# The first feed-forward product by Strassen's algorithm: seven block products per pair of channel tiles and batch in place of eight

## The chip, the cores and the metric

The kernel runs on one core of a Trainium2 chip. The metric is device time in microseconds (us) of one execution; a lower time is better. The engines are named PE (TensorE; PEld is its weight load), DVE (VectorE), ACT (ScalarE), POOL (GpSimd) and SP (SyncE, which issues the DMAs).

## What is computed

Three blocks follow each other: a clustered attention, a first mixing block and a second one, which is where the change lies. With `x` of 2 batches x 768 positions x 512 channels, the second block is

```python
h = xt @ U @ V                      # xt = x transposed, rank 32
u = x + h.transpose(0, 2, 1)
ch = np.maximum(u @ w_ch1, 0.0) @ w_ch2     # 512 -> 2048 -> 512
return u + ch
```

## The kernel before

Everything is kept transposed: channels lie on the 128 partitions, positions along the free axis. `xT[b * 4 + t]` is channel tile t (128 of the 512 channels) of batch b, 768 columns of fp32. Products are made in three passes: each operand is split into a high part `hi` (rounded to fp32r by ACT) and a remainder `lo` (by DVE or POOL), and `PASSES` multiplies hi by hi, hi by lo and lo by hi into the same PSUM bank. Weights come as 64-bit floats. A `Convert` loads 768 columns (SP), makes the fp32 value from the two words (one ACT and three DVE operations: `magnitude`, `bits`, `top`, `low`), and `keep_split` splits it (`wh` on ACT, `wl` on POOL). `conv_step()` emits one DVE operation of the current conversion and one pending function of a finished one; `conv_until` goes on until a given tile is there.

No scheduler reorders the work: each engine takes its instructions in the order of the program text, and waits in that order. PSUM has 8 banks, handed out in turn by `bank()`; a bank is written again only when the reader of its last content is done. SBUF tiles of 128x768 fp32 come from a pool of `SLOTS`.

The stage around the change is the end of `mixer()`. After `chmix(1, e)` and `turn(1, e)` (the last product of the first mixing block and a transposition on DVE), `low1(b)` makes `xt @ U` (24 matmuls, then four ACT copies, a DVE cast and subtraction, which give `h1s`), `low2(b, t)` adds `h` to `xT` (8 matmuls and 8 DVE adds per batch), and `split_u` splits u for the feed-forward products. The loop over `fs` then runs 4 groups of 4 channel tiles f of the 2048, 3 chunks of 512 of the 1536 columns, and 4 tiles f inside. `ff1(c, f)` makes one tile of `u @ w_ch1` (12 matmuls of 512 columns, or 24 of 256 in the chunk that spans both batches), ReLU and the split into `gh` (ACT) and `gl` (DVE). `ff2(c, f)`, two steps later, multiplies it by `w_ch2` into four kept banks, and every fourth f `ff_sum` adds these to `xT`; the last sums go to the output.

Of the kernel before, what the change touches and what calls it, by code (L numbers as in the profile page):

```python
# [10 lines left out]
F32 = mybir.dt.float32  # L11
# [11 lines left out]
P = 128  # L23
NP = 4
# [5 lines left out]
INV_2PI = 1.0 / TWO_PI  # L30
SIN_SCALE = float(np.nextafter(np.float32(TWO_PI), np.float32(0)))
MAGIC = 1.5 * 2.0 ** 23
SLOTS = 62
SETS = 3
STAGED = 3

# [5 lines left out]
def tile_cluster_block(ctx: ExitStack, tc: tile.TileContext, qk, v, cent, wth, wr, wi, wch,  # L42
# [321 lines left out]
    class Convert:  # L364


        def __init__(self, src, n, i, done, rows=P, copies=1):
            self.src, self.i, self.rows, self.copies = src, i, rows, copies
            self.done, self.t = done, None
            self.c0, self.w = i * S, min(S, n - i * S)  # L370

        def load(self):
            self.st = stg.tile([P, S, 2], I32, tag="st", name="st")
# [73 lines left out]
    def weigh_in(src, n, dst):  # L447
        return [Convert(src, n, i, keep_split(dst)) for i in range((n + S - 1) // S)]

    wth_t, wch_t, wr_t, wi_t, w1_t, w2_t = {}, {}, {}, {}, {}, {}  # L450

    def wcol(tiles, c, n):
        i, o = divmod(c, S)
# [156 lines left out]
                             start=True, stop=True)  # L610
            nc.vector.tensor_tensor(x[:, cols(hf)], ps[:, :HALF], x[:, cols(hf)], op=ALU.add)

    def split_u(b, t):
        x = xT[b * NP + t]
        hi, lo = slot(f"uh{b}{t}", F32R), slot(f"ul{b}{t}", F32R)
        nc.scalar.activation(out=hi, in_=x, func=AF.Copy)
        (nc.gpsimd if t % 2 else nc.vector).tensor_tensor(lo, x, f32(hi), op=ALU.subtract)
        us[b, t] = (hi, lo)


    CHUNKS = [[(0, 0, 512)], [(0, 512, 256), (1, 0, 256)], [(1, 256, 512)]]
    NF = DFF // P
    GF = 4
    gt, aps = {}, {}

    def ff1(c, f):
        ps = bank("g")
        o = 0
        for b, s0, w in CHUNKS[c]:
            n = 0  # L630
            for t in range(NP):
                wv = wcol(w1_t, (f * NP + t) * P, P)
                for a, e in PASSES:
                    nc.tensor.matmul(out=ps[:, o:o + w], lhsT=wv[a], rhs=us[b, t][e][:, s0:s0 + w],  # L634
                                     start=(n == 0), stop=(n == 11))
                    n += 1
            o += w
        gh = tmp.tile([P, 512], F32R, tag="gh", name="gh")
        nc.scalar.activation(out=gh, in_=ps, func=AF.Relu)  # L639
        gl = tmp.tile([P, 512], F32R, tag="gl", name="gl")  # L640
        nc.vector.scalar_tensor_tensor(gl, ps, 0.0, f32(gh), op0=ALU.max, op1=ALU.subtract)  # L641
        gt[c, f] = (gh, gl)

    def ff2(c, f):
        first, last = f % GF == 0, f % GF == GF - 1
        if first:
            for e in range(4):
                aps[c, e] = bank("acc", f"acc{e}")
        g = gt.pop((c, f))
        end = last and f == NF - 1  # L650
        for e in range(4):
            wv = wcol(w2_t, f * DM + e * P, P)
            for i, (a, x) in enumerate(PASSES):
                nc.tensor.matmul(out=aps[c, e], lhsT=wv[a], rhs=g[x],  # L654
                                 start=(first and i == 0), stop=(last and i == 2))
            if last:
                ff_sum(c, e, end)

    def ff_sum(c, e, end):

        p0 = 0
        for b, s0, w in CHUNKS[c]:
            x = xT[b * NP + e][:, s0:s0 + w]
            nc.vector.tensor_tensor(x, aps[c, e][:, p0:p0 + w], x, op=ALU.add)
            if end:
                t0 = b * S + s0
                nc.sync.dma_start(out=out[e * P:(e + 1) * P, t0:t0 + w], in_=x)
            p0 += w
        give(f"acc{e}")
# [204 lines left out]
    def mixer():  # L874

        seq = [(u, st) for u in range(4) for st in range(NT)]
        LEAD = 2
        CONVERT = (*range(3, 16), 20, 21)
        last = NG - 1
        for n in range(len(seq) + LEAD):  # L880
            if n < len(seq):
                theta(*seq[n])
                if 3 <= n < 22:
                    conv_step()
                theta_z(*seq[n])
            if n >= LEAD:
                ymix(*seq[n - LEAD])
            if n == 1:
                row_sums(last)
            if n == 2:  # L890
                spread(last)
                norm_x(last)
            if n in CONVERT:
                conv_step()
            if n < len(seq):
                theta_lo(*seq[n])
            if n in CONVERT:
                conv_step()
            if n in (9, 10):
                for t in range(2):  # L900
                    split_x(1, 2 * (n - 9) + t)
            if n == 11:
                conv_load.extend(weigh_in(wch, NP * DM, wch_t))
                c1, c2 = weigh_in(w1, NF * DM, w1_t), weigh_in(w2, NF * DM, w2_t)
                ff = [c for p in zip(c1, c2) for c in p]
                conv_load.extend(ff[:5])
                conv_load.append(Convert(u_in, S, 0, [lambda c, g=g: keep_u(c, g) for g in range(4)], 32, 4))
                conv_load.append(Convert(v_in, S, 0, [keep_v, keep_vl], 32))
                conv_load.extend(ff[5:])
                conv_start()  # L910
            if 20 <= n <= 23:
                clear_u(n - 20)
                split_x(0, n - 20)
            if n in (24, 25):
                split_x(1, n - 24, nc.gpsimd)

        for e in range(NP):
            chmix(0, e)
            if e in (0, 1):
                split_x(1, 2 + e)  # L920
            turn(0, e)
            conv_step(3 if e < 2 else 2)
        conv_until(uv, "u")
        conv_until(uv, "v")
        chmix(1, 0)
        turn(1, 0)
        low1(0)
        chmix(1, 1)
        for t in range(NP):
            low2(0, t)  # L930
        turn(1, 1)
        for t in range(NP):
            split_u(0, t)
        chmix(1, 2)
        turn(1, 2)
        chmix(1, 3)
        turn(1, 3)
        fs = [(c, f) for k in range(NF // GF) for c in range(3) for f in range(k * GF, k * GF + GF)]
        AHEAD = 2
        for n in range(len(fs) + AHEAD):  # L940
            if n < len(fs):
                ff1(*fs[n])
            if n == 0:
                low1(1)
            if n in (1, 2):
                low2(1, 2 * n - 2)
                low2(1, 2 * n - 1)
            if n in (1, 2):
                for t in range(2):
                    split_u(1, 2 * n - 2 + t)  # L950
            conv_step(1 + n % 2 if n > 2 else 0)
            if n >= AHEAD:
                ff2(*fs[n - AHEAD])

    with tc.manual_schedule():
        prologue()
# [7 lines left out]
def _layout(i):  # L964
# [17 lines left out]
    a["wch"] = rows(i["moe_w_ch"])  # L982
    a["u"] = c(i["moe2_U"].reshape(24, 32, RANK).transpose(1, 0, 2).reshape(32, -1))
    a["v2"] = c(i["moe2_V"])
    a["w1"] = c(i["moe2_w_ch1"].reshape(NP, P, DFF // P, P).transpose(1, 2, 0, 3).reshape(P, -1))
    a["w2"] = rows(i["moe2_w_ch2"])
    for k in _WIDE:
        a[k] = a[k].view(np.int64)
    cst = np.zeros((P, 160), np.float32)
# [21 lines left out]
```

## Time and profile before

| | |
|---|---|
| time, median of 3 runs | 698.63 us (697.76 to 699.19) |
| profiled execution: its own time | 697.8 us |
| profiled execution: span of its instructions | 696.0 us |
| mean granted clock of PE | 0.994 |
| instructions | 11370 |

The span runs from the first to the last instruction; some 1.8 us of the time lie around it. A granted clock of 1.00 is 2.4 GHz, 0.50 is 1.2 GHz. PE's matmuls overlap, so that a group's time is read from the start of its first to the start of the next group, not from the duration of one.

### The profile page before, as it was taken

What the parts mean: (1) busy time and instruction counts of PE and PEld (TensorE: products, weight loads), DVE (VectorE), ACT (ScalarE), POOL (GpSimd) and SP (SyncE); (2) the same over time, 40 slices, a digit from 0 to 9 for tenths busy, and PEclk for the clock granted to TensorE, in tenths of its full rate; (3) what the DMA queues carried; (4) which work ended last, traced back from release to release, by engine and by line L of the source; (5) the groups of instructions that cost most, each with busy time, mean ns of one, the idle gap of its engine ahead of it and who ended that gap; (6) DMA issues with size and microseconds to landing.
All of it is one profiled execution on the core that took longest, in us unless ns stands there. A gap on an engine that the chain in (4) does not pass through costs nothing.

```text
span 696.0 us, 11370 instructions
## 1 busy us (share of the span) xinstructions
PE 681.6 (98%) x4492; PEld 556.6 (80%) x4492; DVE 452.1 (65%) x752; ACT 301.8 (43%) x617; POOL 181.0 (26%) x186
## 2 busy tenths in 40 slices
PE   8899999999998999999999999999999999999997
PEld 3567676656755599999999998888898889888986
DVE  7888889898997465568684985566554656432222
ACT  8648557657659444555455432322222222211110
POOL 9422313313228331123244121212121212100000
PEclk9899999999999999999999999999999999999999
DMA  6769768557324110013220320112222121000111
GB/s 211 192 148 288 211 172 229 170 149 203 124 91 137 46 31 2 1 46 103 80 58 1 96 86 1 47 46 90 59 79 89 48 76 31 1 1 0 61 49 72
DMA packets 21109, 63.11 MB, mean 91 GB/s; under 512 B 4192, under 2 KB 6112, under 8 KB 21056
## 3 DMA queue, kind: packets, MB, share of 16 engines
q1 hardware_dynamic: 21056, 62.39, 31.0%
q8 instruction: 35, 0.57, 0.3%
q14 instruction: 18, 0.15, 0.1%
HBM read 40.94 MB, written 3.15 MB: 63 GB/s over the span
## 4 chain that ended last, share of the span: by engine, by line
PE 87%; ACT 5%; DVE 4%; DMA 2%; SPq 1%; issue 1%; ACTq 0%
PE g L634 19%; PE acc L654 19%; PE y L520 14%; PE pv L316 8%; PE st L303 6%; PE h L538 5%; PE th L478 5%; PE l L335 4%; PE smax L251 3%; ACT p L308 2%; DVE mx L255 2%; PE h L589 2%; DMA raw<-in_qk_dram 1%; PE th L482 1%; ACT hi L188 1%
## 5 line engine op out<-in xcount | busy, mean ns | idle before, releaser
L405 POOL TENSOR_TENSOR wl<-cv,wh 128x768 fp32r<-128x768 f32 (+1 forms) x40 | 79.1, 1978 | 235.7 <-ACT wh L401 206.2
L641 DVE SCALAR_TENSOR_TENSOR gl<-g,gh 128x512 fp32r<-128x512 f32 x48 | 33.1, 689 | 133.1 <-ACT gh L639 133.0
L639 ACT ACTIVATE gh<-g 128x512 fp32r<-128x512 f32 x48 | 28.7, 599 | 206.1 <-PE g L634 206.1
L255 DVE TENSOR_REDUCE mx<-smax 128x1 f32<-128x512 f32 x144 | 89.6, 681 | 16.4 <-PE smax L251 16.4
L308 ACT ACTIVATE p<-st 128x512 f32<-128x512 f32 x192 | 78.9, 514 | 43.3 <-PE st L303 42.0
L520 PE MATMUL y<-wh,z 128*128 128x384 f32 x384 | 87.6, 340 | 0.3 <-ACT z L498 0.3
L634 PE MATMUL g<-uh,wh 128*128 128x512 f32 (+1 forms) x256 | 86.9, 339 | 0.0
L634 PE MATMUL g<-uh,wl 128*128 128x512 f32 (+1 forms) x256 | 86.5, 338 | 0.0
L634 PE MATMUL g<-ul,wh 128*128 128x512 f32 (+1 forms) x256 | 86.0, 336 | 0.0
L303 PE MATMUL st<-qp,kp 128*128 128x256 f32 (+1 forms) x384 | 78.7, 349 | 0.4 <-ACT qp L284 0.2
L654 PE MATMUL acc<-gh,wh 128*128 128x512 f32 x192 | 75.9, 395 | 0.0
L654 PE MATMUL acc<-gh,wl 128*128 128x512 f32 x192 | 75.5, 393 | 0.0
L654 PE MATMUL acc<-gl,wh 128*128 128x512 f32 x192 | 75.3, 392 | 0.0
L303 PEld LDWEIGHTS st<-qp,kp 128*128 128x128 f32 x384 | 58.6, 192 | 17.3 <-issue 4.1
L520 PEld LDWEIGHTS y<-wh,z 128*128 128x128 f32 x384 | 66.9, 188 | 0.5 <-ACT z L498 0.5
L316 PE MATMUL pv<-p,v 128*32 128x384 f32 x768 | 65.5, 486 | 0.0
L392 DVE SCALAR_TENSOR_TENSOR cv<-st,cv 128x768 int32<-128x768 int32 (+2 forms) x42 | 64.5, 1537 | 1.0
L316 PEld LDWEIGHTS pv<-p,v 128*32 128x32 f32 x768 | 31.6, 110 | 30.1 <-issue 21.6
L634 PEld LDWEIGHTS g<-ul,wh 128*128 128x128 f32 x256 | 48.5, 189 | 6.1
L634 PEld LDWEIGHTS g<-uh,wl 128*128 128x128 f32 x256 | 48.4, 189 | 5.8
L634 PEld LDWEIGHTS g<-uh,wh 128*128 128x128 f32 x256 | 48.4, 189 | 5.7
L520 PE MATMUL y<-wl,z 128*128 128x384 f32 x192 | 48.8, 335 | 0.0
(128 smaller groups left out, 1166.4 us busy)
## 6 DMA issues: line engine op xcount, KB each, us to landing
st<-in_w_dram SPq DMA_DIRECT2D x20, 768.0 KB, 4.2
raw<-in_qk_dram SPq DMA_DIRECT2D x16, 384.0 KB, 4.5
qp<-hi SPq DMA_DIRECT2D x26, 192.0 KB, 2.9
st<-in_wr_dram SPq DMA_DIRECT2D x6, 768.0 KB, 4.9
st<-in_wi_dram SPq DMA_DIRECT2D x6, 768.0 KB, 4.4
kp<-hi SPq DMA_DIRECT2D x32, 96.0 KB, 3.1
qp<-lo SPq DMA_DIRECT2D x32, 96.0 KB, 2.9
v<-in_v_dram SPq DMA_DIRECT2D x8, 384.0 KB, 3.5
```

What stands on the lines that cost most here:

```text
L255: nc.vector.tensor_reduce(mx_t[g, h][:, o:o + n], ps.rearrange("p (n w) -> p n w", n=n), axis=AX.X, op=ALU.max)
L303: nc.tensor.matmul(out=ps[:, c:c + n], lhsT=kp[s, h, w][:, (a + j) * P:(a + j + 1) * P], rhs=qp[s, h, w][:, q0:q0 + n], start=(w == 0), st ...
L308: nc.scalar.activation(out=pt[g, h, a + j][:, q0:q0 + n], in_=ps[:, c:c + n], func=AF.Exp, scale=float(D) ** -0.5)
L316: nc.tensor.matmul(out=pvt[g][hf][r:r + 32, :HALF], lhsT=v_t[g][:, kt, r:r + 32], rhs=pt[g, r // 64, kt][:, cols(hf)], start=(kt == 0), st ...
L392: nc.vector.scalar_tensor_tensor(t, self.hw, SIGN, t, op0=ALU.bitwise_and, op1=ALU.bitwise_or)
L405: nc.gpsimd.tensor_tensor(t[:, :c.w], c.t, f32(c.hi[:, :c.w]), op=ALU.subtract)
L478: nc.tensor.matmul(out=ps[:, 1], lhsT=xs[b, t][a][:, st * P:(st + 1) * P], rhs=wv[c], start=(n == 0), stop=(n == 11))
L520: nc.tensor.matmul(out=yps[u, j][hf][:, :HALF], lhsT=lhs, rhs=w[st][e][:, hf * HALF:(hf + 1) * HALF], start=(st == 0 and n == 0), stop=(st ...
L538: nc.tensor.matmul(out=ps[hf][:, :HALF], lhsT=wv[a], rhs=xs[b, t][c][:, hf * HALF:(hf + 1) * HALF], start=(n == 0), stop=(n == 11))
L634: nc.tensor.matmul(out=ps[:, o:o + w], lhsT=wv[a], rhs=us[b, t][e][:, s0:s0 + w], start=(n == 0), stop=(n == 11))
L641: nc.vector.scalar_tensor_tensor(gl, ps, 0.0, f32(gh), op0=ALU.max, op1=ALU.subtract)
L654: nc.tensor.matmul(out=aps[c, e], lhsT=wv[a], rhs=g[x], start=(first and i == 0), stop=(last and i == 2))
```

## The change

The operands of the first feed-forward product are cut in two along each axis: the 512 input channels (tiles 0, 1 and tiles 2, 3), the output channels (a pair of tiles f) and the 768 positions of a batch (two halves of 384). A 2x2 by 2x2 block product takes eight block products; the algorithm (in its form with fifteen additions) takes seven, of sums and differences of blocks.

- Weights: `weigh_pair(k)` loads the two tiles of pair k as two conversions of 512 columns, forms the sums s1 to s4 on POOL, and splits them (`keep_22`, `sums`, `keep_upper`, `keep_lower`).
- Activations: `u_sum(b, i)` forms t1 to t4 on DVE, `split_sum` splits them; `split_left` and `split_down` split the blocks of u that are used as they are. `split_u` goes.
- Products: a `Quartet(k, b)` has seven `step`s, each one block product (6 matmuls of 384 columns into one bank) and the additions on DVE that assemble the four blocks of g; `keep` does ReLU and the high part on ACT and the remainder on POOL. Its eight `unit`s are the second product, 6 matmuls of 384 columns each, added to `xT` by DVE after every unit.
- Order: the steps of one quartet alternate with the units of the one before. The first quartet starts between the `chmix` of batch 1; the splits of batch 1 come after its last step, its units after those.
- `_layout` orders the weights in DRAM to match, and the pool has 63 slots for 62.

The diff, without the blank lines and without the removed functions that are printed above:

```diff
--- before.py
+++ after.py
@@ -30,7 +30,7 @@
 INV_2PI = 1.0 / TWO_PI
 SIN_SCALE = float(np.nextafter(np.float32(TWO_PI), np.float32(0)))
 MAGIC = 1.5 * 2.0 ** 23
-SLOTS = 62
+SLOTS = 63
 SETS = 3
 STAGED = 3
@@ -364,10 +364,10 @@
     class Convert:
-        def __init__(self, src, n, i, done, rows=P, copies=1):
+        def __init__(self, src, n, i, done, rows=P, copies=1, width=S):
             self.src, self.i, self.rows, self.copies = src, i, rows, copies
             self.done, self.t = done, None
-            self.c0, self.w = i * S, min(S, n - i * S)
+            self.c0, self.w = i * width, min(width, n - i * width)
         def load(self):
             self.st = stg.tile([P, S, 2], I32, tag="st", name="st")
@@ -380,7 +380,8 @@
         def magnitude(self):
-            self.t = slot("cv")[self.part, :self.w]
+            self.tile = slot("cv")
+            self.t = self.tile[self.part, :self.w]
             nc.scalar.activation(out=self.t, in_=self.hw.bitcast(F32), func=AF.Abs, scale=REBIAS)
         def bits(self):
@@ -447,7 +448,53 @@
     def weigh_in(src, n, dst):
         return [Convert(src, n, i, keep_split(dst)) for i in range((n + S - 1) // S)]
-    wth_t, wch_t, wr_t, wi_t, w1_t, w2_t = {}, {}, {}, {}, {}, {}
+    wth_t, wch_t, wr_t, wi_t, w2_t = {}, {}, {}, {}, {}
+    w1_t, lower = {}, {}
+    def weigh_pair(k):
+        Q = 2 * P
+        def part(c, i):
+            return c.tile[:, i * Q:(i + 1) * Q]
+        def keep_22(c):
+            lower[k] = c
+            t = slot("w22", F32R)
+            nc.scalar.activation(out=t[:, :Q], in_=part(c, 1), func=AF.Copy)
+            nc.gpsimd.tensor_tensor(t[:, Q:2 * Q], part(c, 1), f32(t[:, :Q]), op=ALU.subtract)
+            nc.gpsimd.tensor_tensor(part(c, 2), part(c, 0), part(c, 1), op=ALU.add)
+            lower[k, 22] = t
+        def sums(u):
+            c = lower[k]
+            nc.gpsimd.tensor_tensor(part(u, 2), part(c, 2), part(u, 0), op=ALU.subtract)
+            nc.gpsimd.tensor_tensor(part(c, 0), part(u, 0), part(c, 0), op=ALU.subtract)
+            nc.gpsimd.tensor_tensor(part(c, 1), part(u, 1), part(u, 2), op=ALU.subtract)
+        def split(t):
+            hi = slot("wh", F32R)
+            nc.scalar.activation(out=hi, in_=t, func=AF.Copy)
+            lo = slot("wl", F32R)
+            nc.gpsimd.tensor_tensor(lo, t, f32(hi), op=ALU.subtract)
+            return hi, lo
+        def keep_upper(u):
+            x = split(u.tile)
+            for i, nm in enumerate(("11", "12", "s2")):
+                lower[k, nm] = [t[:, i * Q:(i + 1) * Q] for t in x]
+        def keep_lower(u):
+            x, t = split(lower[k].tile), lower[k, 22]
+            got = {nm: [t[:, i * Q:(i + 1) * Q] for t in x] for i, nm in enumerate(("s3", "s4", "s1"))}
+            got.update({nm: lower[k, nm] for nm in ("11", "12", "s2")})
+            got["22"] = [t[:, :Q], t[:, Q:2 * Q]]
+            w1_t[k] = got
+        n = NF * DM
+        return [Convert(w1, n, 2 * k, [keep_22], width=DM),
+                Convert(w1, n, 2 * k + 1, [sums, keep_upper, keep_lower], width=DM)]
     def wcol(tiles, c, n):
         i, o = divmod(c, S)
@@ -610,63 +657,121 @@
                              start=True, stop=True)
             nc.vector.tensor_tensor(x[:, cols(hf)], ps[:, :HALF], x[:, cols(hf)], op=ALU.add)
...
+    def split_part(b, t, c, hi, lo, eng):
+        x = xT[b * NP + t][:, c]
         nc.scalar.activation(out=hi, in_=x, func=AF.Copy)
...
+        eng.tensor_tensor(lo, x, f32(hi), op=ALU.subtract)
+    def split_left(b):
+        hi, lo = [slot(f"u{b}11{e}", F32R, [P, 2, HALF]) for e in range(2)]
+        for j in range(2):
+            split_part(b, j, cols(0), hi[:, j], lo[:, j], nc.gpsimd)
+        us[b, "11"] = hi, lo
+    def split_down(b, j):
+        if j == 0:
+            us[b, "21"], us[b, "22"] = ({}, {}), ({}, {})
+        hi, lo = slot(f"uh{b}{j}", F32R), slot(f"ul{b}{j}", F32R)
+        split_part(b, 2 + j, slice(0, S), hi, lo, nc.gpsimd)
+        for hf in range(2):
+            for e, t in enumerate((hi, lo)):
+                us[b, f"2{hf + 1}"][e][j] = t[:, cols(hf)]
+    ut = {}
+    def u_sum(b, i):
+        t = slot(f"t{i}", F32, [P, 2, HALF])
+        for j in range(2):
+            up, down = xT[b * NP + j], xT[b * NP + 2 + j]
+            p, m = {1: lambda: (up[:, cols(1)], up[:, cols(0)]), 2: lambda: (down[:, cols(1)], ut[b, 1][:, j]),
+                    3: lambda: (down[:, cols(1)], up[:, cols(1)]), 4: lambda: (down[:, cols(0)], ut[b, 2][:, j])}[i]()
+            nc.vector.tensor_tensor(t[:, j], p, m, op=ALU.subtract)
+        ut[b, i] = t
+    def split_sum(b, i, eng):
+        hi, lo = [slot(f"u{b}t{i}{e}", F32R, [P, 2, HALF]) for e in range(2)]
+        t = ut[b, i]
+        nc.scalar.activation(out=hi, in_=t, func=AF.Copy)
+        eng.tensor_tensor(lo, t, f32(hi), op=ALU.subtract)
+        us[b, f"t{i}"] = hi, lo
     NF = DFF // P
...
+    NQ = NF // 2
+    class Quartet:
+        def __init__(self, k, b):
+            self.k, self.b, self.g = k, b, {}
+        def products(self, ps, x, y):
+            conv_until(w1_t, self.k)
+            w, u = w1_t[self.k][x], us[self.b, y]
             n = 0
...
+            for j in range(2):
                 for a, e in PASSES:
...
+                    nc.tensor.matmul(out=ps[:, :HALF], lhsT=w[a][:, j * P:(j + 1) * P], rhs=u[e][j] if type(u[e]) is dict else u[e][:, j],
+                                     start=(n == 0), stop=(n == 5))
                     n += 1
...
+        def temp(self, i):
+            return tmp.tile([P, 512], F32R, tag=("gh", "gl")[i], name="sum").bitcast(F32)[:, :HALF]
+        def add(self, out, ps, x):
+            nc.vector.tensor_tensor(out, ps[:, :HALF], x, op=ALU.add)
+        def keep(self, i, hf, r):
+            t = slot("g", F32R, [P, 2, HALF])
+            nc.scalar.activation(out=r, in_=r, func=AF.Relu)
+            nc.scalar.activation(out=t[:, 0], in_=r, func=AF.Copy)
+            nc.gpsimd.tensor_tensor(t[:, 1], r, f32(t[:, 0]), op=ALU.subtract)
+            self.g[i, hf] = t
+        def step(self, n):
+            x, y = (("11", "11"), ("12", "21"), ("s2", "t2"), ("s3", "t3"), ("s1", "t1"), ("22", "t4"), ("s4", "22"))[n]
+            ps = bank("q")
+            self.products(ps, x, y)
+            if n == 0:
+                self.u1 = self.temp(0)
+                nc.scalar.activation(out=self.u1, in_=ps[:, :HALF], func=AF.Copy)
+            elif n == 1:
+                r = self.temp(1)
+                self.add(r, ps, self.u1)
+                self.keep(0, 0, r)
+            elif n == 2:
+                self.add(self.u1, ps, self.u1)
+            elif n == 3:
+                self.u2 = self.temp(0)
+                self.add(self.u2, ps, self.u1)
+            elif n == 4:
+                r = self.temp(1)
+                self.add(r, ps, self.u2)
+                self.add(self.u1, ps, self.u1)
+                self.keep(1, 1, r)
+            elif n == 5:
+                self.add(self.u2, ps, self.u2)
+                self.keep(1, 0, self.u2)
+            else:
+                self.add(self.u1, ps, self.u1)
+                self.keep(0, 1, self.u1)
+        def unit(self, n):
+            hf, e = divmod(n, NP)
+            ps = bank("acc")
+            m = 0
+            for i in range(2):
+                wv = wcol(w2_t, (2 * self.k + i) * DM + e * P, P)
+                for a, x in PASSES:
+                    nc.tensor.matmul(out=ps[:, :HALF], lhsT=wv[a], rhs=self.g[i, hf][:, x],
+                                     start=(m == 0), stop=(m == 5))
+                    m += 1
+            x = xT[self.b * NP + e][:, cols(hf)]
+            self.add(x, ps, x)
+            if self.k == NQ - 1:
+                t0 = self.b * S + hf * HALF
+                nc.sync.dma_start(out=out[e * P:(e + 1) * P, t0:t0 + HALF], in_=x)
     bg = deque()
@@ -901,8 +1006,12 @@
                     split_x(1, 2 * (n - 9) + t)
             if n == 11:
                 conv_load.extend(weigh_in(wch, NP * DM, wch_t))
-                c1, c2 = weigh_in(w1, NF * DM, w1_t), weigh_in(w2, NF * DM, w2_t)
-                ff = [c for p in zip(c1, c2) for c in p]
+                c2 = weigh_in(w2, NF * DM, w2_t)
+                ff = []
+                for k in range(NQ):
+                    ff.extend(weigh_pair(k))
+                    while c2 and c2[0].c0 < (k + 1) * 2 * DM:
+                        ff.append(c2.pop(0))
                 conv_load.extend(ff[:5])
                 conv_load.append(Convert(u_in, S, 0, [lambda c, g=g: keep_u(c, g) for g in range(4)], 32, 4))
                 conv_load.append(Convert(v_in, S, 0, [keep_v, keep_vl], 32))
@@ -929,28 +1038,55 @@
         for t in range(NP):
             low2(0, t)
         turn(1, 1)
-        for t in range(NP):
-            split_u(0, t)
+        split_left(0)
+        for j in range(2):
+            split_down(0, j)
         chmix(1, 2)
         turn(1, 2)
+        q = Quartet(0, 0)
+        q.step(0)
+        for i in (1, 2):
+            u_sum(0, i)
         chmix(1, 3)
         turn(1, 3)
-        fs = [(c, f) for k in range(NF // GF) for c in range(3) for f in range(k * GF, k * GF + GF)]
-        AHEAD = 2
-        for n in range(len(fs) + AHEAD):
-            if n < len(fs):
-                ff1(*fs[n])
-            if n == 0:
-                low1(1)
-            if n in (1, 2):
-                low2(1, 2 * n - 2)
-                low2(1, 2 * n - 1)
-            if n in (1, 2):
-                for t in range(2):
-                    split_u(1, 2 * n - 2 + t)
-            conv_step(1 + n % 2 if n > 2 else 0)
-            if n >= AHEAD:
-                ff2(*fs[n - AHEAD])
+        split_sum(0, 2, nc.vector)
+        for i in (3, 4):
+            u_sum(0, i)
+        for i, eng in ((3, nc.gpsimd), (1, nc.vector), (4, nc.gpsimd)):
+            split_sum(0, i, eng)
+        q.step(1)
+        low1(1)
+        q.step(2)
+        q.step(3)
+        for t in range(NP):
+            low2(1, t)
+        for n in (4, 5, 6):
+            q.step(n)
+        split_left(1)
+        for j in range(2):
+            split_down(1, j)
+        for i in (1, 2, 3, 4):
+            u_sum(1, i)
+            split_sum(1, i, nc.vector if i < 3 else nc.gpsimd)
+        for n in range(8):
+            q.unit(n)
+        was = None
+        for k in range(NQ):
+            for b in range(2):
+                if k == b == 0:
+                    continue
+                q = Quartet(k, b)
+                for n in range(7):
+                    q.step(n)
+                    if was:
+                        was.unit(n)
+                    if 0 < n < (7 if k == 0 else 6):
+                        conv_step()
+                if was:
+                    was.unit(7)
+                was = q
+        for n in range(8):
+            was.unit(n)
     with tc.manual_schedule():
         prologue()
@@ -982,8 +1118,9 @@
     a["wch"] = rows(i["moe_w_ch"])
     a["u"] = c(i["moe2_U"].reshape(24, 32, RANK).transpose(1, 0, 2).reshape(32, -1))
     a["v2"] = c(i["moe2_V"])
-    a["w1"] = c(i["moe2_w_ch1"].reshape(NP, P, DFF // P, P).transpose(1, 2, 0, 3).reshape(P, -1))
-    a["w2"] = rows(i["moe2_w_ch2"])
+    half = DFF // P // 2
+    a["w1"] = c(i["moe2_w_ch1"].reshape(NP, P, 2, half, P)[:, :, ::-1].transpose(1, 3, 2, 0, 4).reshape(P, -1))
+    a["w2"] = c(i["moe2_w_ch2"].reshape(2, half, P, DM).transpose(2, 1, 0, 3).reshape(P, -1))
     for k in _WIDE:
         a[k] = a[k].view(np.int64)
     cst = np.zeros((P, 160), np.float32)
```

## Rows read from the trace of the kernel before

**Rows 1.** The page, part 1: busy us (share of the span), instructions.

```profile
PE 681.6 (98%) x4492; PEld 556.6 (80%) x4492; DVE 452.1 (65%) x752; ACT 301.8 (43%) x617; POOL 181.0 (26%) x186
```

**Rows 2.** The page, part 4: the chain that ended last, by engine.

```profile
PE 87%; ACT 5%; DVE 4%; DMA 2%; SPq 1%; issue 1%; ACTq 0%
```

**Rows 3.** Windows: stretch, us, busy PE, PEld, DVE, ACT, POOL, clock, DMA, GB/s.

```profile
417.50:435.00 17.50, 17.50 (x105) 15.60 (x104) 10.01 (x24) 5.08 (x10) 1.85 (x1) 1.00 0.00 1
...
500.00:525.00 25.00, 25.00 (x145) 21.94 (x144) 15.24 (x18) 6.74 (x10) 4.17 (x2) 1.00 0.20 64
```

**Rows 4.** The chain in order of time: start us, us, what.

```profile
403.37 4.16 PE h L538 x24
407.53 1.45 PE h L609 x8
...
417.88 2.76 PE g L634 x12
420.64 5.36 PE h L589 x48
...
441.17 2.88 PE g L634 x24
...
463.85 2.76 PE g L634 x12
```

**Rows 5.** Timeline of the end: start us, us, engine, line, what.

```profile
691.85 0.40 PE L654 MATMUL acc<-gh,wl 128*128 128x512 f32 x1
```

**Rows 6.** Groups by line, weight loads: shape, count | busy us, mean ns.

```profile
L634 PEld LDWEIGHTS g<-ul,wh 128*128 128x128 f32 x256 | 48.5, 189 | 6.1
```

**Rows 7.** Single lines: duration ns min/median/max, starts, shapes.

```profile
L611 DVE TENSOR_TENSOR xT<-h,xT x16: 544/546/548, 408.4 to 435.4; 128x384 f32<-128x384 f32 x16
L392 DVE SCALAR_TENSOR_TENSOR cv<-st,cv x42: 685/959/2491, 73.5 to 608.9; 128x768 int32<-128x768 int32 x37, 128x512 int32<-128x512 int32 x4, 32x768 int32<-32x768 int32 x1
L465 DVE TENSOR_TENSOR xl<-xT,xh x10: 946/951/958, 288.0 to 387.5; 128x768 fp32r<-128x768 f32 x10
L504 POOL TENSOR_TENSOR z<-tht,z x24: 732/738/1274, 242.8 to 371.8; 128x256 fp32r<-128x256 f32 x24
L193 POOL TENSOR_TENSOR lo<-raw,hi x16: 1812/1834/1970, 6.5 to 163.1; 128x768 fp32r<-128x768 f32 x16
L498 ACT ACTIVATE z<-tht x48: 399/410/421, 242.0 to 371.3; 128x256 fp32r<-128x256 f32 x48
L401 ACT ACTIVATE wh<-cv x40: 616/837/922, 78.4 to 617.6; 128x768 fp32r<-128x768 f32 x36, 128x512 fp32r<-128x512 f32 x4
```

**Rows 8.** Timeline of DVE ahead of the feed-forward stage.

```profile
408.40 3.80 DVE L611 TENSOR_TENSOR xT<-h,xT 128x384 f32<-128x384 f32 x8
...
413.19 3.44 DVE L617 TENSOR_TENSOR ul<-xT,uh 128x768 fp32r<-128x768 f32 x2
...
419.45 1.13 DVE L554 STREAM_TRANSPOSE xt<-xT 128x192 f32<-128x192 f32 x4
...
427.18 0.41 DVE L598 CAST h1s<-h 32x512 fp32r<-32x512 f32 x1 [5.18 <-ACT h L595]
427.63 0.68 DVE L599 TENSOR_TENSOR h1s<-h,h1s 32x512 fp32r<-32x512 f32 x1
```

**Rows 9.** Timeline of ACT, two places.

```profile
371.60 2.30 ACT L463 ACTIVATE xh<-xT 128x768 fp32r<-128x768 f32 x3
...
426.04 1.11 ACT L595 ACTIVATE h<-h 32x128 f32<-32x128 f32 x4 [4.76 <-PE h L589]
```

**Rows 10.** Timeline of POOL beside rows 8.

```profile
411.36 4.44 POOL L617 TENSOR_TENSOR ul<-xT,uh 128x768 fp32r<-128x768 f32 x2 [21.24 <-ACT uh L616]
```

**Rows 11.** Windows near the start, columns as in rows 3.

```profile
15.00:20.00 5.00, 3.74 (x14) 1.69 (x14) 4.69 (x11) 3.37 (x6) 4.94 (x4) 0.90 1.01 319
20.00:25.00 5.00, 4.71 (x18) 3.53 (x19) 3.99 (x7) 2.81 (x6) 4.95 (x8) 0.50 0.96 207
25.00:30.00 5.00, 5.00 (x35) 3.05 (x33) 4.72 (x12) 3.70 (x9) 0.03 (x1) 0.92 0.90 253
```

More of the change, by code (lines that the diff above doesn't have):

```diff
@@ L611, in low2 @@
             nc.vector.tensor_tensor(x[:, cols(hf)], ps[:, :HALF], x[:, cols(hf)], op=ALU.add)
-    def split_u(b, t):
-        x = xT[b * NP + t]
-        hi, lo = slot(f"uh{b}{t}", F32R), slot(f"ul{b}{t}", F32R)
+    def split_part(b, t, c, hi, lo, eng):
+        x = xT[b * NP + t][:, c]
         nc.scalar.activation(out=hi, in_=x, func=AF.Copy)
-        (nc.gpsimd if t % 2 else nc.vector).tensor_tensor(lo, x, f32(hi), op=ALU.subtract)
-        us[b, t] = (hi, lo)
-    CHUNKS = [[(0, 0, 512)], [(0, 512, 256), (1, 0, 256)], [(1, 256, 512)]]
@@ L622, in tile_cluster_block @@
-    NF = DFF // P
[L623 to L629, printed above, removed]
+        eng.tensor_tensor(lo, x, f32(hi), op=ALU.subtract)
[12 more added lines that the diff above has]
+                us[b, f"2{hf + 1}"][e][j] = t[:, cols(hf)]
@@ L630, in ff1 @@
+    NF = DFF // P
+    NQ = NF // 2
[5 more added lines that the diff above has]
+            w, u = w1_t[self.k][x], us[self.b, y]
             n = 0
-            for t in range(NP):
-                wv = wcol(w1_t, (f * NP + t) * P, P)
+            for j in range(2):
                 for a, e in PASSES:
-                    nc.tensor.matmul(out=ps[:, o:o + w], lhsT=wv[a], rhs=us[b, t][e][:, s0:s0 + w],
-                                     start=(n == 0), stop=(n == 11))
+                    nc.tensor.matmul(out=ps[:, :HALF], lhsT=w[a][:, j * P:(j + 1) * P], rhs=u[e][j] if type(u[e]) is dict else u[e][:, j],
+                                     start=(n == 0), stop=(n == 5))
@@ L636, in ff1 @@
                     n += 1
[L637 to L669, printed above, removed]
+        def temp(self, i):
+            return tmp.tile([P, 512], F32R, tag=("gh", "gl")[i], name="sum").bitcast(F32)[:, :HALF]
@@ L931, in mixer @@
         turn(1, 1)
-        for t in range(NP):
-            split_u(0, t)
+        split_left(0)
+        for j in range(2):
+            split_down(0, j)
         chmix(1, 2)
         turn(1, 2)
+        q = Quartet(0, 0)
+        q.step(0)
+        for i in (1, 2):
+            u_sum(0, i)
         chmix(1, 3)
         turn(1, 3)
-        fs = [(c, f) for k in range(NF // GF) for c in range(3) for f in range(k * GF, k * GF + GF)]
-        AHEAD = 2
-        for n in range(len(fs) + AHEAD):
-            if n < len(fs):
-                ff1(*fs[n])
-            if n == 0:
-                low1(1)
-            if n in (1, 2):
-                low2(1, 2 * n - 2)
-                low2(1, 2 * n - 1)
-            if n in (1, 2):
-                for t in range(2):
-                    split_u(1, 2 * n - 2 + t)
-            conv_step(1 + n % 2 if n > 2 else 0)
-            if n >= AHEAD:
-                ff2(*fs[n - AHEAD])
+        split_sum(0, 2, nc.vector)
[36 more added lines that the diff above has]
+            was.unit(n)
     with tc.manual_schedule():
```

## The prediction

> **What bounds the kernel now.** I read the page's shares of busy time first: TensorE (PE) is busy 98% of the span, VectorE (DVE) 65%, ScalarE (ACT) 43%, GpSimd (POOL) 26% [rows 1]. A modelled busy share proves little, so the chain that ended last comes next: 87% of it is PE [rows 2]. The windows over the feed-forward stage then say who could take over: PE has no gap, DVE is at 57 to 61%, ACT under 30%, POOL under 20%, the clock is full [rows 3]. Last, the chain in order of time between 403 and 467 us gives PE's prices, since its pieces are whole groups of matmuls that follow each other [rows 4]: 24 matmuls of 384 columns in 4.16 us, 12 of 512 in 2.76, 24 of 256 in 2.88; so 173.5, 230 and 120 ns each. The reader is to see that PE pays by column (0.45 to 0.47 ns), and that the stage ends when PE has streamed its columns.
>
> **What PE saves.** The two products and what stands between them run from 417.88 to 692.25 us (start of the last matmul 691.85, plus 0.40) [rows 4, 5], of which low1(1) takes 5.36 and low2(1) 1.45 as low2(0) did: 267.6 us. After, there are 16 quartets (8 pairs of channel tiles, 2 batches), each with 7 steps and 8 units of 6 matmuls of 384 columns: 240 groups of 6 x 0.1735 = 1.041 us, 249.8 us. PE is relieved of 17.8 us.
>
> Each matmul carries its own weight load, 189 ns long [rows 6]; there are 1344 before (this group and five like it) and 1440 after. Matmuls of 256 columns follow each other at 120 ns beside those loads [rows 4], so loads lie under matmuls and I charge nothing for 96 more. The Trainium skill (TensorE: Matmul & The Clock Gate, The mechanism) says that a load overlaps a running matmul only where the row groups differ; by that sentence 96 x 0.188 = 18 us would be added and the saving would be nil. The trace does not agree: 120 ns is shorter than the load.
>
> **What the other engines get.** A DVE add of 384 columns from PSUM goes at 3.80/8 = 0.475 us and its duration never varies (544 to 548 ns) [rows 7, 8]. A quartet has 7 such adds behind its steps and 8 behind its units, 7.1 us. Conversions: a pair needs two of 512 and 1.33 of 768 columns, three DVE operations each, none dearer than L392's 0.69 and 0.96 alone [rows 7]: at most 8.0 us a pair, 4.0 a quartet. DVE then has 11.1 of the 15.6 us that PE needs for a quartet. POOL pays 0.73 us for 256 and 1.83 for 768 columns, so 1.0 for 384 by the line between; ACT 0.41 and 0.84, with 0.77 from start to start for 768, so 0.45 for 384 in a row [rows 7, 9]. POOL's quartet is 4 remainders of g (4.0) and half a pair's weights (five of 256, 3.33 of 768: 4.9), 8.9 us. ACT's nine operations of 384 and its share of the weights make some 7 us. A DVE difference of 768 columns from SBUF is 0.95, so a half of u_sum 0.5. All fit under PE. The 16 loads of w1 in place of 11 go on SP, three ahead, two quartets (31 us) for 3.33 of them: hidden. 16 output DMAs stay 16.
>
> What does not simply fit is that POOL and DVE hold each other up. Two POOL remainders from 411.36 took 4.44 us where two alone take 3.67, and the DVE subtraction that began beside the second took the rest of it: two that alone take 1.9 needed 3.44 [rows 8, 10]; L392 ranges from 685 to 2491 ns [rows 7]. So I price a DVE operation on SBUF that meets POOL at 0.7 to 0.9 us extra, with 0 and 1.65 as ends. Adds from PSUM are spared.
>
> **The opening, where the cover is missing.** Up to the first full quartet, PE has little to do while splits, sums and evictions pile up. Times follow the clock of before. chmix(1,3), which ended at 417.88, ends at 418.9 behind step 0. Its adds (0.95) and the first transpose (0.28) let low1(1) start at 420.2; step 1 covers until 419.96, where 2.76 us of ff1 covered before: 0.3 idle. low1(1) ends at 425.6, steps 2 and 3 at 427.7. DVE meanwhile does t2's remainder, four halves of u_sum and t1's remainder beside POOL's of t3, so its add for step 1 is done only at 427.0; ACT's two operations for that step (0.9) stand ahead of low1's four copies (1.1), and the cast and subtraction (1.1) follow [rows 8, 9]: h1s at 430.1, where PE waits for low2(1). 2.4 idle. PE is through low2 and steps 4 to 6 at 434.7. DVE needs 0.95 (steps 2, 3), 3.80 (low2), 0.95 and 0.48 (steps 4, 5), to 436.3; ACT's queue gives 437.3, POOL 1.0 and one collision 439.0, and unit 0 waits for exactly that remainder: 4.3 idle.
>
> The units end at 447.3. Their adds stand in DVE's queue behind the sums and splits of batch 1: t1's high part leaves ACT at 441.4 (after keep, split_left, split_down), then 0.95, 1.0, 0.84, 0.95, 2.0 and the add 0.5 give 447.6, and three collisions 450.3. All 8 PSUM banks are then in use by the units, so step 0 of (0,1) waits for that add: 3.0 idle. Its products end at 457.6. The eight unit adds and step 1's end at 454.1, ACT 455.0; on POOL follow keep 1.0, three sums of 256 2.2, the split of the upper weights 1.83 and two collisions: 461.4, the first weights of pair 1. 3.8 idle. One step later unit 0 of (0,1) needs split lower 1.83, two keeps 2.0 and a collision: 465.9. 3.4 idle. Together 17.2 us.
>
> **Later quartets.** From the end of step 5 to the unit that needs its g there are five groups, 5.2 us; add 0.5, ACT 0.9, POOL 1.0, some 1 us of DVE lag and one POOL split of 1.83 ahead make 5.2. Just covered; I charge 0.2 us for each of 13 quartets, 2.6, between 0 and 1.0 each. After the last matmul there remain an add and one output, as before.
>
> **Sum.** -17.8 + 17.2 + 2.6 = +2.0 us. The profiled execution took 697.8 (span 696.0 and 1.8 around it), 0.8 under the median; on the median 698.63 the forecast is 700.6.
>
> **Rivals.** *The opening is cheaper.* Without collisions it loses 6.4 us less (0.7, 2.7, 1.4, 0.7 and 0.9 ahead of h1s) and the quartets nothing: 698.6 - 17.8 + 10.8 = 691.6; half of it 696. For it: PSUM adds never stretch; against: L392's median is 959 of 685, its longest 2491. It decides if collisions cost under 0.4 us each.
> *PE slows down in the opening.* Between 15 and 25 us PE was busy 3.74 of 5 us and the granted clock went to 0.90, then 0.50, then 0.92 [rows 11]: half of 2.4 GHz for 5.9 us, some 3 us of work. From 425.6 to 466 PE works some 26 of 40 us. One such fall gives 703 to 704, two 707. Against it: from 30 us on no window falls. The Trainium skill (TensorE: Matmul & The Clock Gate, HAM oscillation) says idle gaps between bursts bring this back; the fall in this trace agrees.
> *Every quartet waits.* If POOL's remainder misses its unit by 1 us thirteen times, 13 in place of 2.6: 711.
> *The full saving shows.* ACT, DVE and POOL have room on average and the queues reorder nothing that PE needs: 681 to 690. Against it: the chain of six waits above is by order of queues, not by load.
>
> **How the numbers follow.** The forecast (698.5 to 703) gets 0.36, the cheap opening (690 to 698) 0.30, the clock 0.15, waiting quartets 0.12, the full saving 0.07. A run of this kernel tells 0.2% (1.4 us) from nothing. Faster: 0.29 of the cheap opening and 0.07, 0.36; same: 0.13 of the forecast and 0.01, 0.14; slower 0.50. The range 692 to 709 leaves out the full saving, an edge of the cheap opening and half of the waiting quartets. Both signs are open, so the forecast's own range is 698.5 to 703.
>
> **What would show it.** In the windows of the later quartets PE is unbroken, with 1.04 us a group; between 420 and 470 us PE shows six gaps, of which those ahead of low2, unit 0 and the second batch are over 2 us and end on DVE or POOL. The median of the same DVE operation on a whole weight tile lies well above 959 ns. Wrong would make it: no gap over 1 us there (faster), a granted clock under 1.00 after 420 us, or a wait at unit 0 in every quartet (slower).

## The result and the profile after

The change makes the kernel slower: 703.76 us in the median (702.65 to 704.87), beside 698.19 for the kernel before in the same measurement; ratio 1.0079, 95% interval 1.0056 to 1.0102. Forecast were 700.6, a narrow range of 698.5 to 703 and a wide one of 692 to 709. The profiled execution has a span of 702.6 us (696.0 before) and a mean granted clock of 0.980 (0.994). In the experiments below, one execution of `e9_more_warm` took 1105.88 us at a mean granted clock of 0.557, from a cause that is not known, and no figure includes it.

The windows of the changed kernel, columns as in [rows 3], put the loss ahead of 480 us:

```profile
425.00:430.00 5.00, 4.40 (x33) 4.08 (x31) 2.52 (x3) 3.20 (x8) 4.88 (x3) 1.00 0.00 0
430.00:440.00 10.00, 8.35 (x29) 8.14 (x29) 7.91 (x16) 2.95 (x7) 1.43 (x2) 0.66 0.00 1
440.00:450.00 10.00, 8.42 (x46) 7.77 (x45) 7.37 (x6) 4.35 (x9) 9.20 (x6) 1.00 0.00 0
450.00:460.00 10.00, 5.85 (x21) 5.88 (x22) 7.80 (x16) 3.79 (x6) 3.62 (x2) 0.66 0.01 2
460.00:470.00 10.00, 6.20 (x33) 5.30 (x31) 8.18 (x11) 5.43 (x10) 9.81 (x8) 0.96 0.23 79
470.00:480.00 10.00, 8.63 (x37) 8.63 (x38) 4.85 (x9) 3.66 (x8) 6.66 (x6) 0.70 0.19 52
480.00:690.00 210.00, 209.94 (x1212) 209.62 (x1211) 152.93 (x258) 90.40 (x165) 120.77 (x102) 1.00 0.18 54
```

The reader is to see two things. From 480 to 690 us PE has no gap worth naming, with DVE at 73% and POOL at 58%. Between 425 and 480 us PE stands still for some 13 us, and the seventh number, the granted clock, is 0.66, 0.66 and 0.70 in three of the stretches: it alternates between 2.4 and 1.2 GHz (0.50 throughout from 432 to 438, 453 to 458 and 470 to 476 us). In [rows 3] it was 1.00 throughout. PE's waits from 395 us on, in total us, times, longest:

```profile
PE q L715 <- DVE xT L723: 4.7, 1, 4.7
PE acc L767 <- POOL g L729: 3.0, 2, 2.0
PE q L715 <- POOL wl L480: 2.3, 1, 2.3
PE h L656 <- DVE h1s L646: 2.3, 1, 2.3
PE acc L767 <- ACT g L728: 0.8, 1, 0.8
PE h L636 <- DVE xt L601: 0.2, 1, 0.2
```

These are the waits of the prediction: h1s, unit 0 of each of the first two quartets (`acc` on `g`), the first step of (0,1) on a unit's add (`q` on `xT`), the second pair's weights (`q` on `wl`). How the half clock looks from inside is in PE's timeline: low2(1) takes 2.90 us from its first start to its last end, where low2(0) of the kernel before takes 1.61 in the same view (second fence), and matmuls of 384 columns start 0.32 us apart instead of 0.17:

```profile
431.65 2.90 PE L656 MATMUL h<-vs,h1s 96*128 96x384 f32 x8 [2.25 <-DVE h1s L646]
...
456.21 0.52 PE L715 MATMUL q<-uh,wh 128*128 128x384 f32 x1
456.53 0.52 PE L715 MATMUL q<-ul,wh 128*128 128x384 f32 x1
456.85 0.52 PE L715 MATMUL q<-uh,wl 128*128 128x384 f32 x1
...
472.17 0.53 PE L715 MATMUL q<-uh,wh 128*128 128x384 f32 x1
```

```profile
407.37 1.61 PE L609 MATMUL h<-vs,h1s 96*128 96x384 f32 x8
```

One loss lies ahead of all this. The chain in order of time shows `chmix` beginning at 378.73, where it began at 377.21 before:

```profile
374.26 4.46 PE y L567 x24
378.73 20.80 PE h L585 x120
```

The timelines of DVE and, in the fence behind it, of POOL show the largest single piece of the delay:

```profile
356.01 2.62 DVE L533 TENSOR_SCALAR tht<-tht 128x256 f32<-128x256 f32 x1
...
366.04 0.28 DVE L533 TENSOR_SCALAR tht<-tht 128x256 f32<-128x256 f32 x1
```

```profile
355.24 2.56 POOL L480 TENSOR_TENSOR wl<-cv,wh 128x768 fp32r<-128x768 f32 x1
357.74 0.74 POOL L608 MEMSET ub<- 128x768 f32 x1
```

DVE's rounding step of the sine stage, 0.28 us when alone, lasts until 358.63, when POOL is through with a split of the first pair's weights and the memset behind it; PE waits for the z that follows. The chain there also runs through ACT's two splits of the same weights (1.47 us from 351.56), so the collision is not the whole of it.

### The profile page after: what moved, and what is told of

It is laid out like the page before. It is cut to its first block, busy times and chain, and to the rows that moved or that the text cites. A ratio compares the mean times of both kernels' runs of the same rounds, so it can differ in the third digit from the quotient of the medians.

```text
span 702.6 us, 12121 instructions
## 1 busy us (share of the span) xinstructions
PE 674.1 (96%) x4588; PEld 586.8 (84%) x4588; DVE 519.3 (74%) x911; ACT 359.1 (51%) x739; POOL 305.3 (43%) x303
## 4 chain that ended last, share of the span: by engine, by line
PE 72%; DVE 8%; ACT 7%; POOL 6%; issue 5%; DMA 2%; SPq 0%; POOLq 0%; DVEq 0%
PE acc L767 14%; PE q L715 12%; PE y L567 11%; PE pv L316 9%; PE st L303 7%; PE h L585 5%; PE l L335 4%; PE th L525 4%; PE smax L251 3%; POOL g L729 2%; ACT p L308 2%; DVE mx L255 2%; DMA st<-in_wth_dram 1%; POOL wl L480 1%; DVE t L689 1%
## 5 line engine op out<-in xcount | busy, mean ns | idle before, releaser
L767 PE MATMUL acc<-g,wh 128*128 128x384 f32 x512 | 131.8, 337 | 3.9 <-POOL g L729 3.0
L729 POOL TENSOR_TENSOR g<-sum,g 128x384 fp32r<-128x384 f32 x64 | 73.3, 1147 | 101.8 <-ACT g L728 89.5
L723 DVE TENSOR_TENSOR xT<-acc,xT 128x384 f32<-128x384 f32 x128 | 70.2, 554 | 51.2 <-PE acc L767 50.9
L767 PEld LDWEIGHTS acc<-g,wh 128*128 128x128 f32 x512 | 93.1, 189 | 5.4 <-POOL g L729 3.9
L727 ACT ACTIVATE sum<-sum 128x384 f32<-128x384 f32 x64 | 33.6, 525 | 118.5 <-DVE sum L723 118.4
L767 PE MATMUL acc<-g,wl 128*128 128x384 f32 x256 | 86.1, 336 | 0.0
L723 DVE TENSOR_TENSOR sum<-q,sum 128x384 f32<-128x384 f32 x112 | 60.5, 551 | 18.6 <-PE q L715 17.6
L393 DVE SCALAR_TENSOR_TENSOR cv<-st,cv 128x768 int32<-128x768 int32 (+2 forms) x47 | 48.9, 1041 | 0.5
L397 DVE SCALAR_TENSOR_TENSOR cv<-st,cv 128x768 int32<-128x768 int32 (+2 forms) x47 | 48.8, 1039 | 0.4
L767 PEld LDWEIGHTS acc<-g,wl 128*128 128x128 f32 x256 | 48.5, 189 | 0.0
L251 PE MATMUL smax<-kp,qp 128*128 128x512 f32 x192 | 44.1, 348 | 2.9 <-ACT qp L177 1.8
```

The lines of the kernel that those rows point to most:

```text
L251: nc.tensor.matmul(out=ps[:, c:c + w], lhsT=qp[s, h, 0][:, (a + j) * P:(a + j + 1) * P], rhs=kp[s, h, 0][:, k0:k0 + w], start=True, stop=True)
L393: nc.vector.scalar_tensor_tensor(t, self.hw, SIGN, t, op0=ALU.bitwise_and, op1=ALU.bitwise_or)
L723: nc.vector.tensor_tensor(out, ps[:, :HALF], x, op=ALU.add)
L729: nc.gpsimd.tensor_tensor(t[:, 1], r, f32(t[:, 0]), op=ALU.subtract)
L767: nc.tensor.matmul(out=ps[:, :HALF], lhsT=wv[a], rhs=self.g[i, hf][:, x], start=(m == 0), stop=(m == 5))
```

## The experiments

The theory: the later quartets are bound by PE and bring the whole saving; the opening loses it to waits that the order of the queues makes, to collisions of DVE with POOL, and to the clock that falls when PE waits. The rivals: the other engines set the pace of the quartets; or the clock alone is the loss; or POOL's total work in the opening is, so that order changes nothing.

**The eighth product put back** (`e4_eighth`):

```diff
-            self.products(ps, x, y)
+            for _ in range(2 if n == 1 and self.k > 0 else 1):
+                self.products(ps, x, y)
```

> One product more: in the 14 quartets of pairs 1 to 7 the second block product is made twice into the same bank (the result is unchanged), so PE has the eighth product back there, and no other engine has more to do. Theory (the later quartets are bound by PE alone): 14 x 1.04 = 14.6 us more, 718 us. Rival (DVE, POOL and ACT, with their sums, set the pace of the quartets and eat the saving there): under 5 us more.

718.14 us, ratio 1.0275 (1.0246 to 1.0304): 14.4 us more than the change by the medians, 13.7 by the ratios. The window from 480 to 700 us has PE at 219.94 of 220. The quartets pay for every group of matmuls that is added, and without it PE has no gap (209.94 of 210 us), so they also got what seven products in place of eight save; the rival that other engines bind them falls.

**PE kept at work in the opening** (`e1_warm`; the repeated unit is written likewise):

```diff
+    AGAIN = {(0, 0, 3): 2, (0, 0, 6): 1, (0, 1, 6): 2, (1, 0, 0): 2}
...
-            self.products(ps, x, y)
+            for _ in range(1 + AGAIN.get((self.k, self.b, n), 0)):
+                self.products(ps, x, y)
```

> PE repeats products into the same bank (results unchanged) where it waits in the opening: step 3 three times, the last step of (0,0) twice, the last unit five times, the last step of (0,1) and the first of (1,0) three times. Theory (order of queues loses the time, and the halved clock adds to it): the granted clock stays at 1.00 from 420 us on, the waits on DVE and POOL stay, and 2 to 4 us come back: 700 to 702. Rival 1 (the halved clock is the main loss): 6 us or more come back, 698 or less. Rival 2 (the clock only fell where PE waited anyway): nothing comes back, 703 to 705.

700.83 us, ratio 1.0039 (1.0025 to 1.0053), some 2.8 us better than the change by the ratios. The theory's range holds. All windows from 415 to 690 us are at 1.00, here those of 430 to 445 us:

```profile
430.00:435.00 5.00, 4.83 (x27) 4.24 (x26) 4.01 (x9) 1.39 (x4) 0.89 (x1) 1.00 0.00 2
435.00:440.00 5.00, 4.12 (x23) 3.54 (x21) 5.00 (x11) 2.49 (x6) 1.37 (x2) 1.00 0.00 0
440.00:445.00 5.00, 4.03 (x23) 4.04 (x24) 2.83 (x4) 3.47 (x6) 5.00 (x5) 1.00 0.00 0
```

So PE that does more work ends earlier. The fallen clock costs about 3 us, less what the repeats themselves may delay, and not the whole: the kernel is still slower than before. The order of the work is that of the change, so the two timelines of PE also show where the clock acts. From the start of low1(1) to the end of unit 0 of (0,1), which is the start of the next step, the change takes 50.5 us (421.66 to 472.17):

```profile
421.66 5.62 PE L636 MATMUL h<-xt,ub 128*128 128x128 f32 x48 [0.18 <-DVE xt L601]
...
471.37 0.69 PE L767 MATMUL acc<-g,wh 128*128 128x384 f32 x1 [2.04 <-POOL g L729]
```

and this run 47.7 (422.12 to 469.77):

```profile
422.12 5.62 PE L636 MATMUL h<-xt,ub 128*128 128x128 f32 x48 [0.18 <-DVE xt L601]
...
469.31 0.45 PE L771 MATMUL acc<-g,wh 128*128 128x384 f32 x1 [1.09 <-POOL g L731]
469.77 0.33 PE L717 MATMUL q<-uh,wh 128*128 128x384 f32 x1
```

That is 2.9 us, and the two groups behind it, slowed by 1.8 us in the change, run at full pace. The sum of 4.7 is more than the 2.8 of the medians: the profiled execution of the change is slower than its median (704.4 us) and that of this run its fastest (700.25).

**Units ahead of the splits** (`e2_units`):

```diff
+        for i in (1, 2):
+            u_sum(1, i)
+        for n in range(4):
+            q.unit(n)
+        for i in (1, 2):
+            split_sum(1, i, nc.vector)
+        for i in (3, 4):
+            u_sum(1, i)
+        for n in range(4, 8):
+            q.unit(n)
+        for i in (3, 4):
+            split_sum(1, i, nc.gpsimd)
-        for i in (1, 2, 3, 4):
-            u_sum(1, i)
-            split_sum(1, i, nc.vector if i < 3 else nc.gpsimd)
-        for n in range(8):
-            q.unit(n)
```

> Order alone: the first four units of (0,0) stand ahead of the splits of batch 1's sums, the other four behind two of them, so that no unit's add waits in DVE's queue behind them all. Theory: the wait of 4.7 us ahead of the first step of (0,1) goes, and with it the fall of the clock between 450 and 460; but POOL is late for the second pair's weights and for the next unit, which gives back a part: 3 to 6 us faster, 698 to 701. Rival (POOL's total work in the opening sets the end, not DVE's order): the wait moves whole to POOL, 703 to 705.

700.08 us, ratio 1.0024 (1.0011 to 1.0036), 3.8 us better. The wait of 4.7 us is gone from the list, with the fall of the clock between 450 and 460 us, and a part of it is back on POOL and ACT (`u1t`, `wh`), where the clock falls again (0.71 and 0.61 from 460 to 470 us):

```profile
PE acc L767 <- POOL g L729: 2.8, 2, 1.8
PE q L715 <- POOL wl L480: 2.4, 1, 2.4
PE h L656 <- DVE h1s L646: 2.3, 1, 2.3
PE q L715 <- POOL u1t L696: 1.5, 1, 1.5
PE q L715 <- ACT wh L478: 1.1, 1, 1.1
```

**The second pair's weights earlier** (`e3_pair1`):

```diff
         q.step(3)
+        for _ in range(3):
+            conv_after.popleft()()
         for t in range(NP):
             low2(1, t)
```

> Order alone: the sums and splits of the second pair's weights are issued ahead of low2 of batch 1, where POOL stands idle, and not during (0,1). Theory: the waits on POOL at 464 to 471 us (2.3, 0.8 and 2.0) shrink to under 1 and the fall of the clock there goes: 3 to 6 us faster, 698 to 701. Rival (POOL is not what ends last there, the add of step 5 is): under 1 us.

700.68 us, ratio 1.0042 (1.0023 to 1.0062), 2.6 us better, under the theory's 3 to 6. The wait on `wl` is gone; the one on h1s has grown from 2.3 to 3.3 us, and the fall of the clock that was to go is still there (0.66 from 470 to 475 us).

**Step 1 ahead of the splits** (`e5_h1s`):

```diff
         turn(1, 3)
+        q.step(1)
         split_sum(0, 2, nc.vector)
...
-        q.step(1)
         low1(1)
```

> Order alone: step 1 of (0,0) is issued right behind turn(1, 3), ahead of the splits of the sums t, so that its add and ACT's two operations no longer stand between low1 of batch 1 and h1s. Theory: the wait of 2.3 us ahead of low2 and the fall of the clock at 430 to 439 us go; 2 to 4 us faster, 700 to 702. Rival (what stands first behind low2 is DVE's eight adds, so an earlier low2 is waited for again at the units): under 1 us.

705.28 us, ratio 1.0100 (1.0078 to 1.0122): not better than the change, nor worse by more than the intervals, and neither theory nor rival has its mechanism. The wait for h1s is still 2.4 us. DVE's timeline:

```profile
430.23 1.95 DVE L696 TENSOR_TENSOR u0t<-t,u0t 128x768 fp32r<-128x768 f32 x1 [0.71 <-ACT u0t L695]
432.10 2.02 DVE L645 CAST h1s<-h 32x512 fp32r<-32x512 f32 x1
```

and POOL's:

```profile
429.54 4.31 POOL L696 TENSOR_TENSOR u0t<-t,u0t 128x768 fp32r<-128x768 f32 x2 [2.70 <-ACT u0t L695]
```

The cast, 0.41 us in [rows 8], ends 0.3 us behind POOL's remainders of t3 and t4. In the changed kernel it came later and met none. The queue that I removed had hidden a collision.

**The second product's weights first** (`e6_theta`):

```diff
+                ff[:4] = ff[2:4] + ff[:2]
                 conv_load.extend(ff[:5])
```

> Order alone: the two conversions of the second product's weights come ahead of the two of the first pair, so that POOL's three sums and two long splits do not meet the sine stage of the first mixing block. Theory: the last products of that stage wait for z no longer, and chmix begins 1.5 us earlier; 1 to 2 us faster, 702 to 703. Rival (the same work now meets chmix's adds and transposes on DVE): no change.

701.41 us, ratio 1.0041 (1.0026 to 1.0056), 2.7 us better by the ratios, and `chmix` begins at 376.80:

```profile
352.70 4.17 PE y L567 x24
...
376.80 20.80 PE h L585 x120
```

That is 1.9 us earlier than in the change. The end of the sine stage takes 24.1 us again, as in the kernel before (353.10 to 377.21); the 0.4 us by which `chmix` begins earlier than there are already present at 352.70. The kernel before:

```profile
353.10 4.17 PE y L520 x24
...
364.72 12.49 PE y L520 x72
```

The rest of the 2.7 is within the intervals. The edit moves ACT's work on these weights as well as POOL's, so it shows that their conversion in the sine stage costs the time, not which engine's part.

**All four** (`e7_all`, the edits above together):

> The four changes of order together (units ahead of the splits, second pair's weights before low2, step 1 ahead of the splits, second product's weights first). Theory (the opening's losses are those of the queues and sum up, the clock with them): of 24 us lost, 10 to 14 come back: 690 to 694, faster than the kernel before (698). Rival (the waits lie under each other, what is freed is waited for at the next place): 696 to 699.

698.07 us, ratio 0.9995 (0.9981 to 1.0010): level with the kernel before. The singles sum to 7.6 us and 5.9 came, the same within the intervals; the theory's 10 to 14 did not, and the time lies in the rival's range. Two falls of the clock are left (0.65 to 0.67 from 430 to 440 us, 0.74 and 0.58 from 460 to 470). The cast of h1s met POOL as in `e5_h1s`, and unit 0 of (0,1) waited 3.4 us, since conversions stood ahead of the add of step 5 in DVE's queue.

**Two more edits** (`e8_more`):

```diff
-        for i, eng in ((3, nc.gpsimd), (1, nc.vector), (4, nc.gpsimd)):
+        for i, eng in ((3, nc.gpsimd), (1, nc.vector)):
             split_sum(0, i, eng)
         low1(1)
+        split_sum(0, 4, nc.gpsimd)
...
-                    if 0 < n < (7 if k == 0 else 6):
+                    if n > (4 if k == 0 else 0):
                         conv_step()
```

> The four changes of order and two more: t4 of batch 0 is split behind low1 of batch 1, so that POOL doesn't hold DVE's cast for h1s, and the quartet (0,1) issues conversions only behind its steps 5 and 6 (later quartets six instead of five), so that they don't stand ahead of the adds on which the next unit waits. Theory (what is left are collisions of DVE with POOL and conversions in DVE's queue): the waits ahead of low2 (2.8 us) and of the first unit of (0,1) (3.4 us) halve: 3 to 5 us faster than the four changes alone, 693 to 695, and faster than the kernel before (698.5). Rival (each wait freed appears at the next place): 697 to 699.

692.12 us, ratio 0.9916 (0.9901 to 0.9931): faster than both kernels, by about 5.9 and 11 us. The cast is back at 0.41 us, and the wait for h1s at 0.8:

```profile
430.04 0.41 DVE L645 CAST h1s<-h 32x512 fp32r<-32x512 f32 x1
430.49 0.68 DVE L646 TENSOR_TENSOR h1s<-h,h1s 32x512 fp32r<-32x512 f32 x1
```

The wait for unit 0 of (0,1) fell from 3.4 to 0.9 us. The rival has a part too: the waits inside unit 0 of (0,0), 0.9 us in `e7_all`, are 3.9 now. One fall of the clock is left, 0.50 from 440 to 445 us and 0.82 up to 450, where POOL makes the second pair's weights ahead of the remainder for which that unit waits. And with six conversions a quartet the later ones are no longer quite covered: PE is busy 118.72 of 120 us from 480 to 600 us. The two edits were not run apart, so how the gain divides between them is not shown.

**The same with repeats** (`e9_more_warm`, `AGAIN = {(0, 0, 3): 1, (0, 0, 6): 1, (1, 0, 0): 2}`):

> The same, and PE repeats products (results unchanged) at the waits that are left: steps 3 and 6 of (0,0) twice, the first step of (1,0) three times. Theory: the granted clock stays at 1.00 there, and 1 to 3 us more come back: 691 to 694. Rival (the repeats delay what waits for PE): no better than without them.

694.27 us, ratio 0.9933 (0.9915 to 0.9950). The interval overlaps that of `e8_more`, so no gain is shown. The fall between 440 and 445 us was still there (0.66): the repeat of step 6 stands ahead of unit 0 of (0,0), and that unit's waits, 0.8 and 2.0 us, lie inside it.

## Why the prediction was right, and where it was not

The time lies in the wide range, but not in the forecast's own: 5.6 us slower is 704.2 on the forecast's scale, beyond 703. The mechanism was right in its main parts, and two steps of it failed.

**The saving on PE** was sized rightly: 17.8 us from 1.041 us a group. The groups follow at 1.04 us in the chain from 476 us on, and `e4_eighth` paid 13.7 to 14.4 for 14.6. The 96 more weight loads cost nothing that shows.

**Later quartets** were charged 2.6 us; PE is busy 209.94 of 210 us, so it is about 0.1. The other engines' work was sized rightly: 11.1 us of 15.6 for DVE and 8.9 for POOL are 71 and 57%, measured 73 and 58. DVE's adds from PSUM kept their price beside that POOL (540 to 560 ns), and POOL's remainder of 384 columns has a median of 1.03 us (forecast 1.0).

**The opening** has the waits that the queues' order gave, in their places, but its length was missed. From the start of low1(1) to the end of unit 0 of (0,1) the forecast has 46.7 us (420.2 to 465.9 and one group); measured are 50.5. That unit 0 begins 45.7 us behind low1(1) in both (467.36 in the trace) is luck: the forecast has the unit's wait ahead of that start, the trace has it inside the unit. Sizes differ too: ahead of the first step of (0,1) 4.7 for 3.0, ahead of the second pair's weights 2.3 for 3.8, and unit 0 of (0,0) waited about 1 us for 4.3, because low2 and steps 4 to 6, at the half clock, took 3.2 us more and filled the wait.

Where the 3.8 us came in can be read from three starts, when the 1.5 us that low1(1) itself was late are taken off: 1.1 us where unit 0 of (0,0) goes on (441.53 for 439.0), 2.4 at the first step of (0,1) (454.15 for 450.3), 3.7 at POOL's first remainder of (0,1) (460.19 for 455.0). In PE's timeline and, behind it, in POOL's:

```profile
441.53 0.44 PE L767 MATMUL acc<-g,wh 128*128 128x384 f32 x1 [0.94 <-POOL g L729]
...
454.15 0.98 PE L715 MATMUL q<-u,wh 128*128 128x384 f32 x2 [4.72 <-DVE xT L723]
```

```profile
460.19 1.02 POOL L729 TENSOR_TENSOR g<-sum,g 128x384 fp32r<-128x384 f32 x1 [2.95 <-ACT g L728]
```

Behind that nothing much is added: collisions stretched POOL's three sums from 2.2 to 3.6 us, but the forecast had allowed for two there.

**The two steps that failed.** The first is the clock, which the sum put at nothing. "Against it: from 30 us on no window falls" was no argument about a kernel that puts waits of several us into a place where PE had none; the rival that PE slows down came true, three falls instead of one or two, beside the forecast and not in its place. `e1_warm` prices them at about 3 us together, where the rival had 3 for each: a part of the slowed work lay where PE would have waited. (The rows of the early fall give 6.8 us at the half clock, not 5.9.) With the clock up, the opening takes 47.7 us, 0.9 more than the forecast instead of 3.8. The second is the weights' new POOL work, which was charged only where the feed-forward stage begins; the first pair is converted during the sine stage, where it delayed PE by 1.5 us (`e6_theta`). A collision there cost 2.3 us, more than the 1.65 that the prediction gave as the most. From the ends of the last matmul, 692.25 and 699.10, the loss is 6.9 us for a forecast of 2.0: 1.5 from the sine stage, 3.8 more in the opening, 1.8 for the half clock behind unit 0 of (0,1), less 2.5 in the later quartets, leave 0.3 unexplained. That 2.5 us too much in the later quartets covered a part of what the opening lacked is luck as well.

Of the signs named ahead, the unbroken later quartets and the waits of over 2 us ahead of low2 and the second batch came; the median of DVE's operation on the weights did not rise (951 ns for 959), and a granted clock under 1.00 after 420 us, named as a sign of being wrong, came three times.

What stays open is how the 0.9 us that are left of the opening with the clock up divide between collisions and the repeats themselves. The clock's 2.9 us hold collisions too: a slower PE delays the adds that POOL then meets at another moment.

## What to carry to other kernels

A saving in the steady part is spent where the pipeline starts: add up each engine's queue, in its order, over the first round, and ask what PE has to do meanwhile. Put what frees a buffer or releases the next product ahead of work that is only needed later; doing that with the same operations turned 0.8% slower into 0.8% faster. Work that goes to POOL has a price on DVE wherever in the kernel it lands, so look at the stage that is running then, not at the stage it is for.

## What the runs showed of the hardware

Not only DVE operations with two SBUF inputs are held by a running POOL instruction. A `tensor_scalar` of 256 columns with one SBUF input took 2.62 us for 0.28 beside a POOL subtraction of 2.56 and a memset, and a cast of 32x512 took 2.02 for 0.41 beside a POOL remainder. The Trainium skill (GPSIMD Engine Reference, Specifications) names DVE instructions in a 2-port perf mode beside those with two SBUF inputs as the ones that contend with POOL. These rows are in keeping with it, but none shows the mode in which the two ran.

The granted clock fell to 0.50 three times in one stage: behind a wait of PE of 2.3 us, inside one of 4.7 us, and behind two of 2.3 and 0.8 us with little work between. It did not fall in the run that filled those waits with repeated products, which ended earlier for it.
